# High parts of v and of the softmax factors made on ScalarE and stored, in place of masks on VectorE and raw copies

## The chip, the cores and the metric

One core of a Trainium2 chip. The metric is the device time of one execution in microseconds (us), as the median of several runs. Five engines run side by side, each with a queue of its own: TensorE (PE in the profile), VectorE (DVE), ScalarE (ACT), GpSimd (POOL) and SyncE (SP). SyncE only issues DMAs here; GpSimd issues DMAs and clears a few tiles.

## The reference

An attention with compressed keys and values for 8 batches, 8 heads, 576 positions and 64 columns a head, and behind it a block in which 128 of the 576 positions of each batch pass through two matrix products:

```
a    = softmax(phi, over the 576 positions)       # 32 columns a head
k_m  = sum over s of a[s, m] * k[s, d]
v_m  = sum over s of a[s, m] * v[s, d]
attn = softmax(q @ k_m.T / sqrt(64)); x = attn @ v_m, heads side by side (512 columns)
score = x @ w_gate; the 128 rows of largest score of a batch:
out  = x, and on those rows x + sigmoid(score) * (relu(x @ w1) @ w2)
```

## The kernel before

**Staging.** For each batch a chain of VectorE and ScalarE instructions computes the softmax factors a from phi (`softmax`; chain 0 takes batches 0, 2, 4, 6, 7, chain 1 takes 1, 3, 5). `keys` turns them by TensorE into `aS`, splits them, stores the parts to the scratch tensor `aparts`, and sums k_m. `split_v` does the same for v: 32 jobs of 128x576 values, four to a batch, each with a load (L531), a split and a store to the scratch tensor `vparts`. The sum v_m needs exact products from a TensorE that reads float32r, so both operands stand there in two parts, high and low, on partitions of their own.

**Pieces.** v_m is summed by `values` (L739) in 114 pieces of 12 positions. Up to four batches share a piece, 32 partitions each; `FIRST` says at which piece a batch begins, and each runs over 48 pieces: batches 0 to 3 begin at 0, 6, 12, 18, batches 4 to 7 at 48, 54, 60, 66. A piece needs its factors (`a_loader`, L658 on SyncE's queue, into one of three tiles `a_flat`), their widening to blocks of heads (`widener`, four instructions, L717 on VectorE or L719 on ScalarE, into one of two tiles `a_rows`), and its values with both parts (`v_loader`, L694 on the Pool queue, into one of three tiles `v_rows`). From piece 66 on, `values` begins a pair of pieces only when both are there.

**Behind the pieces.** When a batch's last piece is done its sum is turned (L757), and `attention` runs: `centre`, `scores`, `attend` (its first result of the products L929) and `rank`, which finds the 128 rows (L1033). Each of these four is open to one batch at a time. `forward` then gathers the rows, turns them (L1100), multiplies them (L1120, L1138) and writes them back.

**What sets the order.** All jobs are Python generators. `in_order_of_time` runs them against a model of the engines (class `Plan`) and so fixes, ahead of time, the order of the instructions on every queue. A change of one step can so reorder all that follows. On the chip each queue runs in that order, and each instruction waits for what it needs.

**The splits.** In `split_v` the low part of v is v less v with its lowest 12 bits masked away (L548, L550, both VectorE), and it is stored by the Pool queue (L553). The high part isn't computed: `v_copier` copies v itself from HBM to HBM on SyncE's queue (L675, six DMAs in three parts), and TensorE reads it as float32r. `v_loader` waits for both. In `keys` the high part of a batch's factors is a mask too (L593), then the low part a subtraction (L595), once for each half of the heads, and both are stored by the Pool queue (L601).

Of the kernel before, what the change touches and what calls it, by code (L numbers as in the profile page):

```python
# [10 lines left out]
F32 = mybir.dt.float32  # L11
F16 = mybir.dt.float16
F32R = mybir.dt.float32r
BF16 = mybir.dt.bfloat16
I32 = mybir.dt.int32
I16 = mybir.dt.int16
AF = mybir.ActivationFunctionType
ALU = mybir.AluOpType
# [3 lines left out]
P = 128  # L22
NC = 6
T = 12
FIRST = [0, 6, 12, 18, 48, 54, 60, 66]


LOG2E = 1.44269504088896341
# [161 lines left out]
def kernel(  # L190
# [304 lines left out]
    def phi_loader():  # L495
        for b in range(1, B):
            while b > 2 and b - 3 not in turned_away:
                yield lambda: b - 3 in turned_away
            if b == 2:
                yield 20e3  # L500
            load_phi(b)
            yield
# [18 lines left out]
    def split_v():  # L521
        jobs = [(b, g, c) for b in range(B) for c in range(VC) for g in range(NG)]
        asked = deque()

        def view(x, c):
            return x.rearrange("j (c x s) d -> c x j (s d)", c=VC, s=VX)[c]

        def ask():
            b, g, c = jobs[len(done) + len(asked)]
            vb = ex.tile([P, VX * Dh], F32, name="vb", bufs=3)  # L530
            nc.sync.dma_start(  # L531
                out=vb, in_=view(v[g, b % SET, :, first(b) * T:first(b) * T + S], c))
            asked.append((vb, plan.end))

        done, stored = [], [0.0, 0.0]
        yield 8e3
        ask()
        yield
        while len(done) < len(jobs):
            yield max(stored[-2], (8.0 + 7 * len(done)) * 1e3)  # L540
            while len(asked) < 2 and len(done) + len(asked) < len(jobs):
                ask()
            b, g, c = jobs[len(done)]
            vb, at = asked.popleft()
            yield at
            done.append((b, g, c))
            lo = ex.tile([P, VX * Dh], F32, name="vlo", bufs=2)
            nc.vector.tensor_single_scalar(lo.bitcast(I32), vb.bitcast(I32), -4096,  # L548
                                           op=ALU.bitwise_and)
            nc.vector.tensor_sub(lo, vb, lo)  # L550
            yield
            c0 = first(b) * T
            nc.gpsimd.dma_start(out=view(vparts[g, b % SET, :, 0, c0:c0 + S], c), in_=lo)  # L553
            stored.append(plan.end - 2000.0)
            split[b] = split[b][0] + 1, plan.end

# [2 lines left out]
    def keys():  # L559
        for b in range(B):  # L560
            aS = []
            waiting = deque()

            def settle():
                bk, g, c0 = waiting.popleft()
                copy(aS[g][:, :, c0:c0 + 3],
                     bk([PT, 3, P]).rearrange("p c (j m) -> p j c m", m=M))
                bk.give()

            for g in range(NG):  # L570
                while (b, g) not in soft:
                    yield lambda: (b, g) in soft
                yield soft[b, g][1]
                aS.append(ex.tile([PT, NPR, NC, M], F32, name="aS", bufs=2))
                a = soft[b, g][0].rearrange("p (x c) -> p c x", c=NC)
                for c0 in range(0, NC, 3):
                    bk = yield from take()
                    for c in range(3):
                        nc.tensor.transpose(out=bk([PT, 3, P])[:, c], in_=a[:, c0 + c],  # L579
                                            identity=ident)  # L580
                    waiting.append((bk, g, c0))
                    if len(waiting) > 1:
                        settle()
                    yield
            settle()
            turned_away.append(b)
            yield
            c0 = first(b) * T
            made = []
            for g in range(NG):  # L590
                lo = ex.tile([PT, NPR, NC, M], F32, name="alo", bufs=2)
                hi = ex.tile([PT, NPR, NC, M], F32, name="ahi", bufs=2)
                nc.vector.tensor_single_scalar(hi.bitcast(I32), aS[g].bitcast(I32), -4096,  # L593
                                               op=ALU.bitwise_and)
                nc.vector.tensor_sub(lo, aS[g], hi)  # L595
                made.append((lo, hi, plan.end))
            kc = work.tile([P, P], F32, name="kc", bufs=1)
            for g in range(NG):
                yield made[g][2]
                for part, src in enumerate(made[g][:2]):  # L600
                    nc.gpsimd.dma_start(  # L601
                        out=aparts[part, g, b % SET, :, c0:c0 + S]
                            .rearrange("j (p c) m -> p j (c m)", c=NC),
                        in_=src.rearrange("p j c m -> p j (c m)"))
            written[b] = plan.end
            for g in range(NG):
                bk = None
                for h in range(2):
                    while (b, g, h) not in ks:
                        yield lambda: (b, g, h) in ks  # L610
                    kb, at = ks[b, g, h]
                    yield at
                    if bk is None:
                        bk = yield from take()
                        km = bk([P, Dh])
                    for c in range(h * NC // 2, (h + 1) * NC // 2):
                        for j in range(NPR):
                            nc.tensor.matmul(out=km[j * M:(j + 1) * M], lhsT=aS[g][:, j, c],  # L618
                                             rhs=kb[:, j, c % (NC // 2)],
                                             start=(c == 0), stop=(c == NC - 1))  # L620
                    eaten.append(plan.end)
                yield
                copy(kc[:, g * Dh:(g + 1) * Dh], km)
                bk.give()
            bk = yield from take()
            nc.tensor.transpose(out=bk([P, P]), in_=kc, identity=ident)
            yield
            copy(kT[b].rearrange("p j m -> p (j m)"), bk([P, P]))
            bk.give()
            keyed[b] = plan.end  # L630
# [33 lines left out]
            flat.append(max(ends))  # L664
            yield plan.t

    copied = []

    def v_copier():
        yield 12.0 * 1e3  # L670
        edges = [0] + [24, 60] + [COLS // T]
        for c0, c1 in zip(edges, edges[1:]):
            for g in range(NG):
                x, y = (t.rearrange("b j s d -> (b j) (s d)")[:, c0 * T * Dh:c1 * T * Dh] for t in (vparts[g, :, :, 1], v[g]))
                nc.sync.dma_start(out=x, in_=y)  # L675
            copied.extend([plan.end] * (c1 - c0))
            yield plan.t + 40.0 * 1e3

    def v_loader():
        for ch in range(COLS // T):  # L680
            b = live(ch)[-1]
            while split[b][0] < NG * VC or len(copied) <= ch:
                yield lambda: split[b][0] == NG * VC and len(copied) > ch
            yield max(split[b][1], copied[ch])
            while ch - NV >= len(used_up) or len(flat) < ch:
                yield lambda: ch - NV < len(used_up) and len(flat) >= ch
            if ch >= NV:
                yield used_up[ch - NV]
            ends = []
            for g, (r0, r1) in ((g, r) for g in range(NG) for r in slots(ch)):  # L690
                plan.last = None
                src = vparts[g, r0:r1, :, :, ch * T:(ch + 1) * T].rearrange("b j w s d -> (b j w) (s d)")
                n = (r1 - r0) * NPR * 2
                nc.gpsimd.dma_start(  # L694
                    out=v_rows[ch % NV].bitcast(F32)[32 * r0 + g:32 * r1:2, g]
                        .rearrange("p s d -> p (s d)"),
                    in_=src.unsqueeze(1).to_broadcast([n, 2, T * Dh]))
                ends.append(plan.end)
            v_loaded.append(max(ends))
            yield plan.t  # L700
# [26 lines left out]

    def values():
        for ch in range(COLS // T):
            last = min(ch + 1 - ch % 2, COLS // T - 1) if ch >= 66 else ch  # L730
            while last >= min(len(widened), len(v_loaded)):
                yield lambda: last < min(len(widened), len(v_loaded))
            yield max(widened[last], v_loaded[last])
# [423 lines left out]
    def load_weights():  # L1157
# [24 lines left out]
    in_order_of_time(plan, [  # L1182
        (lambda: ahead(0), chain([[0, 2, 4, 6, 7], [1, 3, 5]][0], 0)), (lambda: ahead(1), chain([[0, 2, 4, 6, 7], [1, 3, 5]][1], 1)),
        (0.5 * 1e3, keys()), (0.0 * 1e3, split_v()),
        (0.0, phi_loader()), (0.0, k_loader()), (0.0, q_loader()), (0.0, a_loader()), (0.0, v_loader()), (0.0, v_copier()), (0.0, widener()),
        (0.0 * 1e3, values()), (0.0 * 1e3, attentions(0)), (0.0 * 1e3, attentions(1)),
        (None and None * 1e3, forward(B * nt)), (0.0, load_weights())])

# [51 lines left out]
```

## Time and profile before

| | us |
|---|---|
| median of 3 runs | 726.15 (725.95 to 727.72) |
| the profiled execution | 725.9 |
| its span in the trace | 724.0 |
| busy: VectorE | 567.1 |
| busy: TensorE | 465.0 |
| busy: ScalarE | 392.6 |
| busy: GpSimd | 216.6 |

The shares are means over stages with different limits. What counts is which engine is full in which stretch, and what the others wait for there. A queue with idle time costs nothing as long as nobody waits for it.

### The profile page before, as it was taken

How to read it: one execution, taken by the hardware profiler on the slowest of the kernel's cores; microseconds unless marked ns; L12 is line 12 of the kernel's file. 1: busy time of each engine (PE TensorE's matmuls, PEld its weight loads, DVE VectorE, ACT ScalarE, POOL GpSimd, SP SyncE). 2: the span in 40 equal slices, each digit the busy share in tenths (PEclk: the TensorE clock that was granted, in tenths of full speed). 3: DMA queues.
4: the chain of work that ended last, by engine and by line, in shares of the span. 5: the costliest groups of instructions: out<-in, count | busy, mean ns of one | idle time of the engine just before them, and what ended most of it. 6: DMA issues, size and time to landing. Idle time of an engine off the chain costs nothing.

```text
span 724.0 us, 18212 instructions
## 1 busy us (share of the span) xinstructions
PE 465.0 (64%) x7130; PEld 382.4 (53%) x7130; DVE 567.1 (78%) x990; ACT 392.6 (54%) x710; POOL 216.6 (30%) x387
## 2 busy tenths in 40 slices
PE   0002156074262474765668878999999999899990
PEld 0002045073261463654557677887878887686660
DVE  4999999999989996877988789879635877978000
ACT  3544664586462995867964376564646573243100
POOL 5001321431333241442332524244344331211100
PEclk9999999999975696998898999999999999999995
DMA  9613696776677686888987977887655543212000
GB/s 297 222 47 119 188 319 192 243 210 204 206 224 237 210 272 207 236 271 279 269 267 223 304 238 212 253 258 231 204 178 160 170 147 117 78 52 76 30 14 19
DMA packets 68109, 139.12 MB, mean 192 GB/s; under 512 B 13648, under 2 KB 46416, under 8 KB 67792
## 3 DMA queue, kind: packets, MB, share of 16 engines
q1 hardware_dynamic: 48752, 67.60, 31.4%
q0 software_dynamic: 19264, 70.28, 29.8%
q8 instruction: 58, 0.95, 0.6%
q14 instruction: 35, 0.29, 0.1%
HBM read 107.41 MB, written 41.62 MB: 206 GB/s over the span
## 4 chain that ended last, share of the span: by engine, by line
PE 33%; DMA 17%; DVE 13%; ACT 9%; SPq 6%; issue 5%; POOL 1%; ACTq 0%; DVEq 0%
PE acc L739 11%; DMA a_flat<-aparts 10%; ACT a_rows L719 6%; SPq L658 6%; PE acc L1138 4%; PE bank L1120 4%; PE acc L1120 3%; PE bank L1138 3%; DMA qb<-in_qT 2%; DMA aparts<-ahi 2%; DMA w<-in_w 2%; PE bank L904 1%; PE bank L1028 1%; PE bank L918 1%; DVE marks L1009 1%
## 5 line engine op out<-in xcount | busy, mean ns | idle before, releaser
L739 PE MATMUL acc<-v_rows,a_rows 32*128 32x256 f32 x4608 | 219.8, 312 | 97.8 <-ACT a_rows L719 77.8
L739 PEld LDWEIGHTS acc<-v_rows,a_rows 32*128 32x128 f32 x4608 | 201.5, 214 | 117.5 <-ACT a_rows L719 85.5
L719 ACT ACTIVATE a_rows<-a_flat,block_of 128x384 fp32r<-128x384 f32 x325 | 174.1, 604 | 91.2 <-PE acc L739 40.0
L694 POOL DMA_DIRECT2D v_rows<-vparts x228 | 128.5, 567 | 222.0 <-PE acc L739 199.5
L717 DVE TENSOR_SCALAR a_rows<-a_flat,block_of 128x384 fp32r<-128x384 f32 x131 | 49.9, 420 | 46.8 <-DMA a_flat<-aparts 31.2
L579 PE MATMUL bank<-ident,ph 128*96 128x128 f32 x96 | 20.4, 359 | 73.3 <-DVE ph L476 73.3
L553 POOL DMA_DIRECT2D vparts<-vlo x32 | 18.6, 582 | 122.1 <-DVE vlo L550 122.1
L579 PEld LDWEIGHTS bank<-ident,ph 128*96 128x96 f32 x96 | 14.3, 190 | 77.1 <-issue 59.5
L618 PE MATMUL bank<-kb,aS 96*32 96x64 f32 x768 | 22.5, 282 | 42.9 <-DMA kb<-in_k 42.9
L618 PEld LDWEIGHTS bank<-kb,aS 96*32 96x32 f32 x768 | 17.5, 148 | 48.3 <-issue 27.2
L1009 DVE SCALAR_TENSOR_TENSOR marks<-row,tg,wide 128x576 bf16<-128x576 f32 x40 | 32.7, 818 | 7.4 <-ACT row L993 5.7
L962 POOL DMA_DIRECT2D out<-xj x24 | 16.4, 683 | 61.4 <-DVE less L1014 25.6
L1120 PE MATMUL bank<-xeT,w 128*128 128x128 f32 x256 | 32.8, 281 | 1.7 <-ACT xeT L1104 1.7
L1120 PE MATMUL acc<-xeT,w 128*128 128x128 f32 x256 | 31.7, 279 | 2.0 <-ACT xeT L1104 2.0
L1120 PEld LDWEIGHTS bank<-xeT,w 128*128 128x128 f32 x256 | 29.9, 192 | 4.2 <-ACT xeT L1104 2.1
L1005 ACT ACTIVATE marks<-row,tg 128x576 bf16<-128x576 f32 x40 | 31.0, 776 | 1.8
L1120 PEld LDWEIGHTS acc<-xeT,w 128*128 128x128 f32 x256 | 29.6, 192 | 4.1 <-ACT xeT L1104 3.0
L1138 PE MATMUL bank<-w,hT 128*128 128x512 f32 x64 | 30.4, 605 | 0.0
L1138 PE MATMUL acc<-w,hT 128*128 128x512 f32 x64 | 29.5, 600 | 0.0
L473 DVE SCALAR_TENSOR_TENSOR ph<-rh,sm,ph 128x576 f32<-128x576 f16 x32 | 26.0, 813 | 2.8 <-ACT rh L462 2.5
L968 DVE TENSOR_TENSOR prod<-xj,wg 128x512 f32<-128x512 f32 x40 | 27.4, 686 | 0.4
L971 DVE TENSOR_REDUCE four<-prod 128x128 f32<-128x512 f32 x40 | 27.2, 681 | 0.6
(163 smaller groups left out, 924.9 us busy)
## 6 DMA issues: line engine op xcount, KB each, us to landing
v_rows<-vparts POOLq DMA_DIRECT2D x156, 192.0 KB
a_flat<-aparts SPq DMA_DIRECT2D x312, 48.0 KB
vb<-in_v SPq DMA_DIRECT2D x32, 288.0 KB
kb<-in_k SPq DMA_DIRECT2D x32, 288.0 KB
vparts<-vlo POOLq DMA_DIRECT2D x32, 288.0 KB
qb<-in_qT SPq DMA_DIRECT2D x16, 576.0 KB
out<-xj POOLq DMA_DIRECT2D x16, 512.0 KB
vparts<-in_v SPq DMA_DIRECT2D x2, 2592.0 KB
```

The lines of the kernel that those rows point to most:

```text
L579: nc.tensor.transpose(out=bk([PT, 3, P])[:, c], in_=a[:, c0 + c], identity=ident)
L618: nc.tensor.matmul(out=km[j * M:(j + 1) * M], lhsT=aS[g][:, j, c], rhs=kb[:, j, c % (NC // 2)], start=(c == 0), stop=(c == NC - 1))
L658: nc.sync.dma_start(out=a_flat[ch % NF][32 * r0 + 2 * t + g:32 * r1:4] .rearrange("p s m -> p (s m)"), in_=src[:, ch * T * M:(ch + 1) * T ...
L694: nc.gpsimd.dma_start(out=v_rows[ch % NV].bitcast(F32)[32 * r0 + g:32 * r1:2, g] .rearrange("p s d -> p (s d)"), in_=src.unsqueeze(1).to_b ...
L717: nc.vector.tensor_scalar_mul(ar[:, :, j], src, block_of[:, j:j + 1])
L719: nc.scalar.activation(ar[:, :, j], src, AF.Copy, scale=block_of[:, j:j + 1])
L739: nc.tensor.matmul(out=accs[b % SET][:, :2 * P].rearrange("p (r g d) -> p r g d", g=NG, d=Dh), lhsT=ar[p, s].rearrange("p j m -> p (j m)") ...
L968: nc.vector.tensor_mul(prod, x[:, c], wg)
L1005: nc.scalar.activation(sign, row, AF.Sign, bias=g, scale=-1.0, accum_out=less[:, c:c + 1])
L1009: nc.vector.scalar_tensor_tensor(out=cmp, in0=row, scalar=g, in1=wide[:, off:off + S], op0=ALU.is_equal, op1=ALU.mult, accum_out=equal[:, ...
L1120: nc.tensor.matmul(out=bk([P, 4, P])[:, f, :n], lhsT=w1_sb[d][:, (f0 + f) * P:(f0 + f + 1) * P], rhs=xeT[:, d, :n], start=(d == 0), stop=( ...
L1138: nc.tensor.matmul(out=ps[:n], lhsT=hT[:, f, :n], rhs=w2_sb[f], start=(f == 0), stop=(f == KF - 1))
```

## The change

`split_v` writes the high part of v by a ScalarE copy into a float32r tile, subtracts it from v in place on VectorE, and stores both parts by the Pool queue. The mask, the low tile and the copies from HBM to HBM are gone, and `v_loader` waits for the split alone. Jobs of v are due 6.5 us apart instead of 7. In `keys` the high part of the factors is a ScalarE copy into float32r, and the subtraction is planned as a step of its own, after the copies of both halves. Batch 1 begins at piece 10 instead of 6, batch 5 at 58 instead of 54; the count of pieces stays 114. Pieces are begun in pairs from piece 60 instead of 66.

```diff
-FIRST = [0, 6, 12, 18, 48, 54, 60, 66]
+FIRST = [0, 10, 12, 18, 48, 58, 60, 66]
...
-            yield max(stored[-2], (8.0 + 7 * len(done)) * 1e3)
+            yield max(stored[-2], (8.0 + 6.5 * len(done)) * 1e3)
...
-            lo = ex.tile([P, VX * Dh], F32, name="vlo", bufs=2)
-            nc.vector.tensor_single_scalar(lo.bitcast(I32), vb.bitcast(I32), -4096,
-                                           op=ALU.bitwise_and)
-            nc.vector.tensor_sub(lo, vb, lo)
+            hi = ex.tile([P, VX * Dh], F32R, name="vhi", tag="vlo", bufs=2)
+            copy(hi, vb)
+            yield
+            nc.vector.tensor_sub(vb, vb, hi.bitcast(F32))
             yield
             c0 = first(b) * T
-            nc.gpsimd.dma_start(out=view(vparts[g, b % SET, :, 0, c0:c0 + S], c), in_=lo)
+            for w, src in enumerate((vb, hi.bitcast(F32))):
+                nc.gpsimd.dma_start(out=view(vparts[g, b % SET, :, w, c0:c0 + S], c), in_=src)
...
-                hi = ex.tile([PT, NPR, NC, M], F32, name="ahi", bufs=2)
-                nc.vector.tensor_single_scalar(hi.bitcast(I32), aS[g].bitcast(I32), -4096,
-                                               op=ALU.bitwise_and)
+                hi = ex.tile([PT, NPR, NC, M], F32R, name="ahi", bufs=2)
+                copy(hi, aS[g])
+                made.append((lo, hi.bitcast(F32), plan.end))
+            for g in range(NG):
+                lo, hi, at = made[g]
+                yield at
                 nc.vector.tensor_sub(lo, aS[g], hi)
-                made.append((lo, hi, plan.end))
+                made[g] = lo, hi, plan.end
...
-    copied = []
-
-    def v_copier():
...
-            while split[b][0] < NG * VC or len(copied) <= ch:
-                yield lambda: split[b][0] == NG * VC and len(copied) > ch
-            yield max(split[b][1], copied[ch])
+            while split[b][0] < NG * VC:
+                yield lambda: split[b][0] == NG * VC
+            yield split[b][1]
...
-            last = min(ch + 1 - ch % 2, COLS // T - 1) if ch >= 66 else ch
+            last = min(ch + 1 - ch % 2, COLS // T - 1) if ch >= 60 else ch
```

## Rows read from the trace of the kernel before

**Rows 1.** Stretches: busy us (count) PE, PEld, DVE, ACT, POOL; clock, DMA, GB/s.

```profile
24.00:229.00 205.00, 71.66 (x819) 62.33 (x819) 197.27 (x244) 111.53 (x156) 48.42 (x81) 0.95 0.63 193
244.00:378.00 134.00, 86.24 (x2077) 76.72 (x2070) 114.77 (x161) 105.18 (x179) 47.30 (x83) 0.85 0.83 254
378.00:456.00 78.00, 63.95 (x1276) 53.03 (x1261) 64.89 (x157) 45.84 (x108) 29.77 (x53) 0.91 0.79 243
456.00:672.00 216.00, 209.33 (x2775) 166.89 (x2776) 158.82 (x394) 108.15 (x245) 70.66 (x118) 1.00 0.50 158
672.00:706.00 34.00, 32.39 (x177) 22.24 (x175) 1.82 (x3) 3.58 (x6) 2.96 (x3) 1.00 0.07 24
```

**Rows 2.** VectorE, 20 to 240 us, its largest wait: us in total, times, longest.

```profile
DVE vlo L548 <- DMA vb<-in_v: 2.5, 2, 1.7
```

**Rows 3.** Order of time round batch 3: start, us, engine, line, operation, idle before.

```profile
228.05 0.95 DVE L595 TENSOR_TENSOR alo<-aS,ahi 96x768 f32<-96x768 f32 x1
...
230.01 0.87 POOL L601 DMA_DIRECT2D aparts<-ahi  x1
...
241.25 4.16 ACT L719 ACTIVATE a_rows<-a_flat,block_of 128x384 fp32r<-128x384 f32 x8 [1.02 <-DMA a_flat<-aparts]
...
243.44 2.94 PE L739 MATMUL acc<-v_rows,a_rows 32*128 32x256 f32 x48 [13.12 <-ACT a_rows L719]
```

**Rows 4.** Instructions grouped by shape: count, busy us, mean ns of one, idle before.

```profile
L553 POOL DMA_DIRECT2D vparts<-vlo x32 | 18.6, 582 | 122.1 <-DVE vlo L550 122.1
...
L548 DVE TENSOR_SCALAR vlo<-vb 128x576 int32<-128x576 int32 x32 | 14.7, 458 | 2.5 <-DMA vb<-in_v 2.5
...
L462 ACT ACTIVATE rh<-ph,sm 128x576 f16<-128x576 f32 x16 | 11.4, 762 | 4.9 <-DVE sm L458 4.9
...
L394 ACT ACTIVATE rh<-ph 128x1152 int16<-128x1152 f32 x8 | 9.3, 1162 | 33.7 <-DVE ph L392 33.7
...
L593 DVE TENSOR_SCALAR ahi<-aS 96x768 int32<-96x768 int32 x16 | 8.8, 549 | 0.0
```

**Rows 5.** VectorE's masks alone in the front: L548, then L593, busy us (count).

```profile
24.00:229.00 205.00, 13.31 (x29) 0.95 0.63 193
...
24.00:230.00 206.00, 4.40 (x8) 0.94 0.63 193
```

**Rows 6.** DMA queues of the page: packets, MB, share of 16 engines' span.

```profile
q1 hardware_dynamic: 48752, 67.60, 31.4%
q0 software_dynamic: 19264, 70.28, 29.8%
```

**Rows 7.** Order of time: sums read (L757), an attention's products, last rank and round.

```profile
378.88 0.26 ACT L757 ACTIVATE turned<-acc 128x128 f32<-128x128 f32 x1
...
402.76 0.28 ACT L757 ACTIVATE turned<-acc 128x128 f32<-128x128 f32 x1 [1.13 <-PE acc L739]
...
421.59 0.19 DVE L929 TENSOR_SCALAR rd<-bank 128x40 f32<-128x40 f32 x1
...
561.32 0.26 ACT L757 ACTIVATE turned<-acc 128x128 f32<-128x128 f32 x1
...
580.52 0.26 ACT L757 ACTIVATE turned<-acc 128x128 f32<-128x128 f32 x1
...
671.24 0.16 DVE L1033 TENSOR_SCALAR idx<-bank 128x1 int32<-128x1 f32 x1 [1.77 <-PE bank L1028]
...
690.07 0.60 PE L1100 MATMUL acc<-ident,xe 128*128 128x128 f32 x4
```

**Rows 8.** Waits of SyncE's queue at the loads of v, 20 to 245 us.

```profile
SPq L531 <- DVE vlo L550: 56.7, 12, 24.7
...
SPq L531 <- DMA vparts<-in_v: 13.1, 2, 8.1
```

**Rows 9.** Wait of the Pool queue for pieces, 20 to 245 us.

```profile
POOL v_rows L694 <- PE acc L739: 31.2, 8, 9.1
```

**Rows 10.** The page's first part: busy us, share of the span, instructions.

```profile
PE 465.0 (64%) x7130; PEld 382.4 (53%) x7130; DVE 567.1 (78%) x990; ACT 392.6 (54%) x710; POOL 216.6 (30%) x387
```

More of the change, by code (lines that the diff above doesn't have):

```diff
@@ L665, in a_loader @@
             yield plan.t
-    copied = []
-    def v_copier():
[L670 to L677, printed above, removed]
     def v_loader():
@@ L1184 @@
         (0.5 * 1e3, keys()), (0.0 * 1e3, split_v()),
-        (0.0, phi_loader()), (0.0, k_loader()), (0.0, q_loader()), (0.0, a_loader()), (0.0, v_loader()), (0.0, v_copier()), (0.0, widener()),
+        (0.0, phi_loader()), (0.0, k_loader()), (0.0, q_loader()), (0.0, a_loader()), (0.0, v_loader()), (0.0, widener()),
         (0.0 * 1e3, values()), (0.0 * 1e3, attentions(0)), (0.0 * 1e3, attentions(1)),
```

## The prediction, made before the changed kernel was run

> **What bounds the kernel now.** I read the stretches of the span first [rows 1]. They show three regimes. From 24 to 229 us VectorE is busy 197.27 of 205 us, TensorE only 71.66 and ScalarE 111.53. From 244 to 456 us nothing is full: TensorE is busy 86.24 of 134 and then 63.95 of 78 us. From 456 to 706 us TensorE is busy 209.33 of 216 and 32.39 of 34 us: it works off a backlog, and what it finds to do is always there. So the end is set by the time at which TensorE becomes full, and that by how early the front gets through.
>
> What holds the front is read from the waits of VectorE between 20 and 240 us: its largest wait of all there adds to 2.5 us [rows 2]. VectorE is simply full, with the softmax of the factors, with the splitting of v and of the factors into parts. The order of time round batch 3 shows how that reaches TensorE [rows 3]: the last low part of the factors of batch 3 is subtracted at 228.05, its parts leave on the Pool queue at 230.01, the widening begins at 241.25, and at 243.44 TensorE begins piece 18, the first that has batch 3, after 13.12 us of waiting. Pieces before it run as soon as their batch is there and wait for the next one, so piece 18 is the gate of the front. Everything behind it (96 pieces, eight attentions, eight rounds of the block) follows on.
>
> **VectorE's masks go.** By shape, a mask of v is 0.458 us (L548, 32 times) and a mask of a factor tile 0.549 us (L593, 16 times) [rows 4]. In the stretch that ends with batch 3's factors, 29 of the first (13.31 us) and 8 of the second (4.40 us) lie on the full VectorE [rows 5]: together 17.7 us. The new spacing of the jobs of v, 6.5 for 7 us, doesn't raise the 29: the front ends earlier by about as much as the jobs are nearer (211 - 8 over 6.5 is 31.2 and 229 - 8 over 7 is 31.6, by the due times alone). The subtractions stay as they are.
>
> **ScalarE gets the copies.** No row of before is a plain copy of these shapes. For 128x576 the bounds are half of the 1.162 us that 1152 columns take (L394), 0.58, and the 0.762 us of the scaled conversion of 576 columns (L462) [rows 4]. I take 0.70, nearer to L462, which has the same width. For 96x768 they are two thirds of 1.162, 0.775, and 0.762 plus 192 columns of the slope between the two rows (0.400 / 576 each), 0.895; I take 0.84. In the front that is 29 x 0.70 + 8 x 0.84 = 27.0 us (23.0 to 29.3), so that ScalarE goes from 111.5 of 205 to some 138.5 of 188 us, 74%: room, but less of it. Over the whole kernel it is 32 x 0.70 + 16 x 0.84 = 35.8 us added on ScalarE, for 14.7 + 8.8 = 23.5 us removed from VectorE [rows 4]: 12.3 us more of engine time. A copy of v also waits for its load, and behind it on ScalarE stand widenings and softmax steps; that the loads come late cost VectorE 2.5 us so far [rows 2], and I leave that as it is.
>
> Each subtraction now waits for a ScalarE result. Behind a waiting subtraction on VectorE stand the softmax steps of both chains, and for these ScalarE and the next batch wait. The bound is zero if the planner always puts other work between, as it does now, and otherwise what such waits cost now: all idle time of VectorE in the front is 205 - 197.3 = 7.7 us [rows 1], and softmax has some 50 steps there that take a ScalarE result (ten in each of some five batches), so at most 0.15 us each, 5.7 us for 37 more. I take 2.0, since the named waits are so small [rows 2]. For the factors of batch 3 the mask in line with its subtraction becomes a copy on another queue: from 1 us earlier to 2 us later; I take 1.0 later. Piece 18 then starts 17.7 - 2.0 - 1.0 = 14.7 us earlier, near 229.
>
> A rule that speaks against this is in the Trainium skill, Perfetto Trace Analysis, section Optimizing Scalar/DVE Operations: where VectorE has a fast mode for an operation it is the quicker place, though with VectorE saturated some work may go to ScalarE. By the first half alone the kernel would come out 12.3 us later, at 738.4; by the second it gains. The trace agrees with the second for the front, and leaves it open behind 244 us.
>
> **Raw copies go, stored high parts come.** Six copies from HBM to HBM on SyncE's queue give way to 32 more stores of 288 KB on the Pool's. The copies move 114 pieces x 12 rows x 64 x 4 bytes x 32 = 11.2 MB, the stores 9.4 MB. SyncE's queue has 31.4% of the 16 engines' span for 67.60 MB, 3.36 us a MB; the Pool's 29.8% for 70.28 MB, 3.07 us a MB [rows 6]. That is -37.7 + 29.0 = -8.7 us of transfer time, nearly all inside a front that is 63% loaded [rows 1]: I count it at nothing, between -2 and +2 us, as no wait of VectorE rests on it. On the Pool, issuing 32 more stores at 0.582 us [rows 4] is 18.6 us; Pool has 48.42 of 205 us busy there [rows 1], and the issue time is hidden by that. Its order isn't free, see the second rival.
>
> **Behind piece 18.** Between 244 and 378 us VectorE (114.77 of 134) and ScalarE (105.18 of 134) are nearly equal [rows 1]. Four batches of factors are split there: 8 x 0.549 = 4.4 us leave VectorE, 8 x 0.84 = 6.7 us come to ScalarE. The bounds are -4.4 and +6.7; I take nothing, as the planner gives each widening to the freer of the two. From 456 us on TensorE has the same work, so it ends earlier by what it begins earlier.
>
> **The pieces.** Batch 1 runs over pieces 10 to 57 and batch 5 over 58 to 105, four later than before. At the front that is covered by the waits for batches 2 and 3. Its price is at the ends of those batches: batch 1's sum is ready at 378.88 and batch 2's, six pieces on, at 402.76, so four pieces are 15.9 us; for batch 5 (561.32, and 580.52 six pieces on) 12.8 us [rows 7]. Cover for batch 1: its attention begins its products at 421.59, when batch 0's has let go, while the sum was there 42.7 us before. Cover for batch 5: the last batch's rank is known at 671.24, and TensorE only takes its round at 690.07, 18.8 us later [rows 7]. Both covers exceed the delays, so zero; without them it would be 15.9 and 12.8 us. Waiting for pairs from piece 60 instead of 66 moves six pieces and I count zero, within one piece's time either way (15.9 / 4 = 4.0 us).
>
> **The sum.** 725.9 us for the profiled execution (span 724.0 and 1.9 around it) - 14.7 = 711.2. The median is 726.15, 0.25 above that execution: 711.5 for the median.
>
> **The rivals.** First, the gain is lost before 456 us. Batch 1's delay of 15.9 us cancels the 14.7 us at its attention, and if TensorE's fullness hangs on that attention and not on the pieces, the end is 726.15 - 14.7 + 15.9 = 727.4 at most; half of it, 719, if batch 0 fills in. For it speaks the 64 of 78 us that TensorE is busy just then [rows 1]; against it the cover of 42.7 us.
>
> Second, slower: the queues couple. The tile of v is now overwritten by its own low part and is free only when the Pool's store has landed; the next load of v into it stands on SyncE's queue, and behind that stand the loads of the factors for the pieces. Now the same load waits for the subtraction, 56.7 us in the front [rows 8], while the Pool's queue waits 31.2 us for pieces on TensorE, in eight waits of up to 9.1 us [rows 9]. If those eight fall between a store and the SyncE load that needs it, and all reach the path, the time is 726.15 - 17.7 + 31.2 = 739.7. It decides once more than 17.7 us of the 31.2 come ahead of the loads for pieces 12 and 18. Against it: three tiles of v give a store nearly three jobs' time to land, and with the raw copies a wait of 13.1 us leaves SyncE [rows 8]. The Trainium skill, DMA: Bandwidth & Descriptors, section Issuing engine by pattern, would keep plain stores on SyncE's path, which it calls generally faster; the rows' 3.07 us a MB don't show that.
>
> Third, ScalarE becomes the bound: its copies wait behind widenings that wait for TensorE, and the subtractions with them. With all 12.3 us of added engine time on the path the time is 726.15 + 12.3 = 738.4; it decides where ScalarE, at 78% between 244 and 378 us, is later than VectorE at most pieces. With the 5.7 us and 2 us bounds of the front alone it would be 726.15 - 17.7 + 7.7 = 716.2, still faster.
>
> **How the numbers follow.** Forecast, 702 to 720: 0.70. The first rival 0.14, of which 0.04 at 720 to 724, 0.08 within 0.3% and 0.02 above. The second 0.11, the third 0.05, of which 0.01 each within 0.3%. About 0.3%, 2.2 us, is what a measurement of this kernel can tell from no change. Faster 0.74, same 0.10, slower 0.16. The low end of the range is all 23.5 us of removed masks with nothing given back, 702.6, rounded to 702; the high end takes in the first rival and a quarter of the second, 730.
>
> **What would show it.** After: VectorE busy near 567.1 - 23.5 = 543.6 us and ScalarE near 392.6 + 35.8 = 428.4 [rows 10]; piece 18 beginning near 229 us; TensorE full from about 442; batch 3's factors leaving near 215. Wrong, if piece 18 starts at 240 or later (second rival: SyncE's loads of v waiting for the Pool's stores), if it starts early and TensorE fills no earlier (first rival), or if VectorE shows waits for ScalarE's copies of more than 6 us (third).

## The result, and the profile after

The changed kernel takes 706.76 us as the median of 4 runs (705.59 to 709.69), beside 726.93 us (725.95 to 729.38) for the kernel before: a ratio of 0.972 with an interval of 0.968 to 0.977, or 20.2 us less. The forecast was 711.5: the direction is right, and 4.7 us are missing from it. The two profiled executions differ by as much: span 703.9 for 724.0 us. Executions more than 1.5% above the fastest of the same kernel are left out of every median and ratio from here on.

Stretches of the kernel after, with the columns of [rows 1]: busy us (and count) of TensorE, its weight loads, VectorE, ScalarE and GpSimd, then clock, DMA share and GB/s.

```profile
24.00:215.00 191.00, 74.58 (x771) 65.13 (x771) 180.83 (x210) 132.74 (x191) 63.79 (x110) 1.00 0.65 208
...
244.00:378.00 134.00, 86.07 (x2032) 75.25 (x2031) 109.38 (x166) 97.66 (x167) 46.23 (x82) 0.85 0.84 255
378.00:442.00 64.00, 50.20 (x1047) 41.76 (x1042) 48.08 (x121) 36.68 (x84) 26.52 (x47) 0.89 0.80 244
442.00:660.00 218.00, 210.97 (x2834) 167.91 (x2835) 165.32 (x409) 109.46 (x250) 71.85 (x118) 1.00 0.52 161
```

The three regimes are still there, only earlier. Up to 215 us VectorE is busy 180.83 of 191 us, and from 442 us on TensorE is full, 210.97 of 218, where it was full from 456 [rows 1]. Over the same time, from 440 to 460 us, it is busy 19.15 of 20 us, and 16.49 in the kernel before.

The order of time round batch 3 in the kernel after, to be held against [rows 3]:

```profile
213.89 0.94 DVE L599 TENSOR_TENSOR alo<-aS,ahi 96x768 f32<-96x768 f32 x1
...
218.32 0.68 POOL L605 DMA_DIRECT2D aparts<-ahi  x1
...
228.82 3.65 ACT L711 ACTIVATE a_rows<-a_flat,block_of 128x384 fp32r<-128x384 f32 x7 [1.16 <-DMA a_flat<-aparts]
...
231.00 1.23 PE L731 MATMUL acc<-v_rows,a_rows 32*128 32x256 f32 x16 [8.12 <-ACT a_rows L711]
```

The last subtraction begins at 213.89 for 228.05 us, 14.2 earlier; piece 18 at 231.00 for 243.44, 12.4 earlier. In a second profiled execution of the changed kernel (e8, below) piece 18 is at 228.63, 14.8 earlier.

From the gate the gain goes through to the end almost whole. Order of time in the kernel before, its last product, its last result and its last store:

```profile
705.57 0.20 PE L1191 MATMUL bank<-good,ones 128*1 128x8 f32 x2
705.68 0.75 DVE L1144 SCALAR_TENSOR_TENSOR ye<-acc,gr,xe 128x512 f32<-128x512 f32 x1 [14.65 <-PE acc L1138]
...
706.71 0.97 POOL L1149 DMA_INDIRECT out<-ye,idx  x1 [14.41 <-DVE any_bad L1197]
```

And in the kernel after, with the last rank ahead of it:

```profile
662.70 0.16 DVE L1025 TENSOR_SCALAR idx<-acc 128x1 int32<-128x1 f32 x1 [0.55 <-PE acc L1020]
...
694.69 0.96 POOL L1141 DMA_INDIRECT out<-ye,idx  x1 [14.42 <-DVE any_bad L1189]
```

The last store is issued 12.0 us earlier. But the span is 20.1 us shorter. The other 8.1 us lie behind the last store: from its issue to the end of the span are 724.0 - 706.71 = 17.3 us before and 703.9 - 694.69 = 9.2 us after. The instructions of the line that ends the program, on the Pool queue (durations ns min/median/max, then first and last start in us), say what it is. The profile calls them DRAIN; what they wait for, no row shows. Before:

```profile
L1236 POOLq DRAIN  x3: 46/108/9133, 713.8 to 723.4; - x3
```

After:

```profile
L1228 POOLq DRAIN  x3: 46/108/2441, 700.6 to 703.6; - x3
```

The longest of three drains of the Pool queue took 9.133 us before and takes 2.441 us now: 6.7 of the 8.1 us. Of the remaining 1.4 us, 1.2 are that the drains begin 5.9 us behind the last store for 7.1.

**The new work in size.** Instructions of the kernel after by shape: count, busy us, mean ns, idle before and what ended it, as [rows 4].

```profile
L550 DVE TENSOR_TENSOR vb<-vb,vhi 128x576 f32<-128x576 f32 x32 | 24.0, 749 | 0.6 <-ACT vhi L548 0.5
L548 ACT ACTIVATE vhi<-vb 128x576 fp32r<-128x576 f32 x32 | 21.5, 672 | 17.0 <-DMA vparts<-vhi 10.9 <-DMA vb<-in_v 4.7 <-issue 1.2
...
L594 ACT ACTIVATE ahi<-aS 96x768 fp32r<-96x768 f32 x16 | 12.5, 834 | 0.0
```

VectorE's whole wait for the copies of v is 0.5 us, once. The first part of the page and its queues, as [rows 10] and [rows 6]:

```profile
PE 467.3 (66%) x7130; PEld 384.7 (55%) x7130; DVE 550.2 (78%) x962; ACT 412.6 (59%) x738; POOL 234.3 (33%) x419
...
q0 software_dynamic: 21952, 79.72, 34.4%
q1 hardware_dynamic: 48432, 56.39, 27.8%
```

### The profile page after: what moved, and what is told of

Same layout as the page of the kernel before. It is cut to its first block, busy times and chain, and to the rows that moved or that the text cites. A ratio compares the mean times of both kernels' runs of the same rounds, so it can differ in the third digit from the quotient of the medians.

```text
span 703.9 us, 18360 instructions
## 1 busy us (share of the span) xinstructions
PE 467.3 (66%) x7130; PEld 384.7 (55%) x7130; DVE 550.2 (78%) x962; ACT 412.6 (59%) x738; POOL 234.3 (33%) x419
## 3 DMA queue, kind: packets, MB, share of 16 engines
q0 software_dynamic: 21952, 79.72, 34.4%
## 4 chain that ended last, share of the span: by engine, by line
PE 39%; DMA 17%; DVE 17%; ACT 9%; issue 8%; SPq 6%; POOL 2%; ACTq 0%; DVEq 0%; POOLq 0%
PE acc L731 14%; DMA a_flat<-aparts 8%; PE bank L1112 6%; SPq L662 6%; DMA kb<-in_k 4%; PE acc L1130 4%; PE bank L1130 4%; ACT a_rows L711 3%; PE bank L910 2%; DMA qb<-in_qT 2%; PE acc L1112 2%; DVE ph L473 1%; DVE vb L550 1%; PE bank L1020 1%; PE acc L896 1%
## 5 line engine op out<-in xcount | busy, mean ns | idle before, releaser
L731 PE MATMUL acc<-v_rows,a_rows 32*128 32x256 f32 x4608 | 222.7, 314 | 92.5 <-ACT a_rows L711 67.9
L731 PEld LDWEIGHTS acc<-v_rows,a_rows 32*128 32x128 f32 x4608 | 204.8, 216 | 111.9 <-ACT a_rows L711 76.7
L711 ACT ACTIVATE a_rows<-a_flat,block_of 128x384 fp32r<-128x384 f32 x305 | 164.9, 605 | 106.6 <-DMA a_flat<-aparts 54.1
L709 DVE TENSOR_SCALAR a_rows<-a_flat,block_of 128x384 fp32r<-128x384 f32 x151 | 57.6, 420 | 61.5 <-DMA a_flat<-aparts 29.0
L554 POOL DMA_DIRECT2D vparts<-vb x32 | 18.7, 585 | 113.4 <-DVE vb L550 108.1
L580 PEld LDWEIGHTS bank<-ident,ph 128*96 128x96 f32 x96 | 14.7, 191 | 76.2 <-issue 58.0
L1112 PE MATMUL bank<-xeT,w 128*128 128x128 f32 x384 | 48.1, 280 | 3.4 <-ACT xeT L1096 2.8
L1112 PEld LDWEIGHTS bank<-xeT,w 128*128 128x128 f32 x384 | 44.5, 192 | 7.1 <-ACT xeT L1096 4.2
L548 ACT ACTIVATE vhi<-vb 128x576 fp32r<-128x576 f32 x32 | 21.5, 672 | 17.0 <-DMA vparts<-vhi 10.9
L963 DVE TENSOR_REDUCE four<-prod 128x128 f32<-128x512 f32 x40 | 27.2, 680 | 0.6
L1136 DVE SCALAR_TENSOR_TENSOR ye<-acc,gr,xe 128x512 f32<-128x512 f32 x4 | 3.0, 747 | 30.0 <-PE acc L1130 30.0
```

The source lines that it names most:

```text
L709: nc.vector.tensor_scalar_mul(ar[:, :, j], src, block_of[:, j:j + 1])
L711: nc.scalar.activation(ar[:, :, j], src, AF.Copy, scale=block_of[:, j:j + 1])
L731: nc.tensor.matmul(out=accs[b % SET][:, :2 * P].rearrange("p (r g d) -> p r g d", g=NG, d=Dh), lhsT=ar[p, s].rearrange("p j m -> p (j m)") ...
L1112: nc.tensor.matmul(out=bk([P, 4, P])[:, f, :n], lhsT=w1_sb[d][:, (f0 + f) * P:(f0 + f + 1) * P], rhs=xeT[:, d, :n], start=(d == 0), stop=( ...
```

## The experiments

Theories before the runs. A: relief of the full VectorE up to piece 18 is the gain, as predicted. B: it is the copies from HBM to HBM, whose traffic went away. C: it is the new places of batches 1 and 5 (`FIRST`) and of the pairs. The 8 us behind the last store needed a theory of their own. They ran in three groups, each beside runs of the kernel before on the same chip, whose medians are 728.50 us for e1 to e4, 726.54 for e5 to e8 and 728.74 for e9 to e12. Ratios are against the kernel before in the same group; they aren't the plain quotients of these medians. Where an experiment says "in unchanged order", its instruction was added without the planner knowing of it, so that all queues keep their order; elsewhere the planner made a new one.

**e1 to e4: one part at a time, re-planned.** e1 is the kernel before with the ScalarE parts alone.

```diff
-            nc.vector.tensor_single_scalar(lo.bitcast(I32), vb.bitcast(I32), -4096, ...)
-            nc.vector.tensor_sub(lo, vb, lo)
+            hi = ex.tile([P, VX * Dh], F32R, name="vhi", tag="vlo", bufs=2)
+            copy(hi, vb)
+            yield
+            nc.vector.tensor_sub(vb, vb, hi.bitcast(F32))
...
+                copy(hi, aS[g])
```

> The kernel before with the high parts made on ScalarE and nothing else: the low part is subtracted in place and stored, the raw copies from HBM to HBM stay, batches, spacing and pairs stay. Here TensorE still reads the raw v as its high part, which need not be the rounded one that was subtracted; that part of the sum is changed. Theory one (VectorE's masks held the front): piece 18 starts 10 to 14 us earlier than the 243.44 us of before, and the last instruction of work comes as much earlier, so 711 to 717 us. Theory two (the copies from HBM to HBM held it): 724 to 730 us, piece 18 later than 240 us. Theory three (8 us of the gain lie behind the last store, in the Pool queue's drain at the end of the program, 9.1 us before and 2.4 after): the drain here tells whether it goes with the stores; with the 9.1 us drain the time is 714 to 716, with the short one 706 to 709.

e2 is the changed kernel with the masks on VectorE again, stored as they are.

```diff
-            copy(hi, vb)
+            nc.vector.tensor_single_scalar(hi.bitcast(I32), vb.bitcast(I32), -4096, ...)
...
-                copy(hi, aS[g])
+                nc.vector.tensor_single_scalar(hi.bitcast(I32), aS[g].bitcast(I32), -4096, ...)
```

> The changed kernel with the high parts masked on VectorE again, in tiles of their own, and still stored; everything else as changed. Theory one: piece 18 back at 240 to 246 us (231.00 after), the time 718 to 724 us with a short drain. Theory two (copies and stores carry the gain): 705 to 710 us, piece 18 at 231 to 234 us. Theory three: the drain stays near 2.4 us if the 32 further stores on the Pool queue decide it, so that the time is 8 us under what piece 18 alone would give.

e3 is the changed kernel with the copies of v from HBM to HBM back, in place of the stored high part.

```diff
-            for w, src in enumerate((vb, hi.bitcast(F32))):
-                nc.gpsimd.dma_start(out=view(vparts[g, b % SET, :, w, c0:c0 + S], c), in_=src)
+            nc.gpsimd.dma_start(out=view(vparts[g, b % SET, :, 0, c0:c0 + S], c), in_=vb)
...
+    def v_copier(): ...   # as before
```

> The changed kernel with the raw copies from HBM to HBM back in place of the stored high parts of v (TensorE again reads the raw v as its high part, so that part of the sum is changed). Theory one: within 3 us of the changed kernel up to the last store, piece 18 at 229 to 234 us. Theory two: piece 18 at 238 us or later, 716 us or more. Theory three: the drain is near 9 us if it goes with the number of stores on the Pool queue, and the time is 713 to 717 us although piece 18 is early; near 2.4 us otherwise and 704 to 709 us.

e4 is the kernel before once more.

> The kernel before, once more, for the drain at the end of the program alone. If it belongs to the kernel: 8.5 to 9.5 us again, 725 to 729 us. If it is an accident of one execution: anything from 2 us, and the span shorter by as much.

Measured: e1 735.10 us, ratio 1.009 (1.006 to 1.013); e2 1.014 (1.005 to 1.022) from two executions of 727.55 and 734.29 us; e3 740.22, 1.017 (1.010 to 1.023); e4 724.61, with the drain of 9.133 us again. In e1 and e3 the sum v_m is a changed one, as their texts say; the work on the queues is as described. Neither ScalarE's copies without the stores (e1, e3) nor the stores without ScalarE's copies (e2) gain anything; together they gain 20 us. So neither A nor B holds as a term that can be added by itself. The table shows where, for the kernels whose order was planned anew, one profiled execution a row (start of piece 18, the last subtraction of the jobs of v, how many of these begin behind the start of piece 18, the time from there to piece 48, the last store issued, and the time from there to the end of the span):

| | piece 18 | last job of v | jobs behind piece 18 | piece 18 to 48 | last store | behind it |
|---|---|---|---|---|---|---|
| before | 243.4 | 240.7 | 0 | 113.1 | 706.7 | 17.3 |
| before (e4) | 243.0 | 240.6 | 0 | 108.8 | 705.4 | 17.4 |
| after | 231.0 | 230.0 | 0 | 116.0 | 694.7 | 9.2 |
| after (e8) | 228.6 | 227.2 | 0 | 112.2 | 695.4 | 9.4 |
| e1 | 231.6 | 284.2 | 6 | 126.7 | 716.2 | 17.6 |
| e2 | 238.6 | 269.2 | 3 | 122.7 | 715.7 | 10.1 |
| e3 | 234.3 | 277.3 | 5 | 128.4 | 722.1 | 17.8 |
| e10 | 225.4 | 239.9 | 2 | 124.2 | 702.6 | 9.4 |
| e11 | 222.5 | 284.1 | 7 | 131.8 | 721.2 | 8.8 |

In e1 the gate opens 11.9 us earlier, as A says: VectorE's relief is real with the copies in place. But the jobs of v now end at 284 us, 53 us behind the gate instead of ahead of it, and the stretch from piece 18 to 48 takes 13.6 us more than before. What TensorE waits for in that stretch of e1 (us in total, times, longest):

```profile
PE acc L742 <- ACT a_rows L722: 39.0, 16, 13.7
PE bank L621 <- DMA kb<-in_k: 9.4, 4, 3.3
PE acc L742 <- DMA v_rows<-vparts: 8.9, 2, 7.0
```

And from piece 18 to 48 in the kernel before:

```profile
PE acc L739 <- ACT a_rows L719: 36.9, 19, 13.1
PE acc L739 <- DVE a_rows L717: 10.2, 2, 9.7
...
PE bank L618 <- DMA kb<-in_k: 1.8, 1, 1.8
```

For widenings TensorE waits no longer in e1 (39.0 + 2.2 on VectorE for 47.1), but for the transfers of keys and of values 18.3 us where the kernel before has 1.8. The transfers alone don't make the difference, though. In the same stretch of the changed kernel (e8) they are waited for too:

```profile
PE acc L731 <- ACT a_rows L711: 27.2, 12, 9.2
PE acc L731 <- DMA v_rows<-vparts: 6.6, 2, 3.8
PE bank L622 <- DMA kb<-in_k: 4.9, 2, 3.3
```

That is 11.5 us, and the stretch is no longer than before. Against e8, e1 waits 6.8 us more for transfers and 11.4 more for widenings (39.0 + 2.2 for 27.2 + 2.6). Nor is the whole loss in that stretch: from piece 48 to the last store e1 takes 357.9 us, for 350.1 in the kernel before and 354.6 in e8. So late jobs of v became a suspect, and so did the price of the copies, which a plan of its own can hide. The next runs kept the order.

**e5 and e6: masks alone and copies alone, in unchanged order.** e5 is the changed kernel with 48 masks on VectorE whose result nobody reads. e6 has the six copies of v, to a scratch tensor that nobody reads, issued on SyncE's queue at the 1st, 7th and 13th job. By the trace that is in pairs from 7.3, 66.0 and 118.5 us; the kernel before issues its own from 3.9, 12.5 and 92.0 us, so e6 prices them at other places. e7 has one copy of 48 KB in their place, to see whether such a copy by its mere presence lengthens the end; e8 is the changed kernel as it is.

```diff
+            dead = ex.tile([P, VX * Dh], I32, name="dead", bufs=1)
+            tc.nc.vector.tensor_single_scalar(dead, vb.bitcast(I32), -4096, op=ALU.bitwise_and)
             nc.vector.tensor_sub(vb, vb, hi.bitcast(F32))
...
+                dead = ex.tile([PT, NPR, NC, M], I32, name="deada", bufs=1)
+                tc.nc.vector.tensor_single_scalar(dead, aS[g].bitcast(I32), -4096, op=ALU.bitwise_and)
                 nc.vector.tensor_sub(lo, aS[g], hi)
```

> The changed kernel with the 48 masks back on VectorE as dead work: each writes a tile that nothing reads, right ahead of its subtraction, and the planner isn't told, so the order of all other instructions on every queue is that of the changed kernel. It takes apart the cost of the masks from that of another order. Theory one (VectorE full in the front, what is saved there goes to the end): piece 18 starts 29 x 0.46 + 8 x 0.55 = 17.7 us less the 9 us that VectorE stood idle there, so 9 to 18 us after the 231.00 of the changed kernel, and the time is 716 to 725 us. Rival (the gain is the new order's and the copies', the masks were hidden): piece 18 within 4 us, the time 705 to 711 us.

```diff
+            for c0, c1, n in ((0, 24, 1), (24, 60, 7), (60, COLS // T, 13)):   # e7: ((0, 1, 1),)
+                if len(done) == n:
+                    for g0 in range(NG):                                       # e7: range(1)
+                        ...   # x = vraw[g0], y = v[g0], columns c0 to c1
+                        tc.nc.sync.dma_start(out=x, in_=y)
```

> The changed kernel with the six copies of v from HBM to HBM back as dead transfers into a scratch tensor that nothing reads, issued on SyncE's queue with the first, seventh and thirteenth job of v; the planner isn't told, so the order of all other instructions is that of the changed kernel. Theory of the order (the copies cost the kernels that have them 8 us in the drain at the end, and nothing else by their traffic): piece 18 and piece 48 within 3 us of 231.0 and 347.0, the last store of the block within 3 us of 694.7, then 17 to 18 us to the end instead of 9.2, so 713 to 717 us. Rival (the traffic itself delays the front): piece 18 at 236 us or later, 718 us or more. Second rival (the drain goes with the number of stores on the Pool queue): 9 to 10 us behind the last store.

> The changed kernel with one short dead copy from HBM to HBM (one piece of v, 48 KB, on SyncE's queue) and nothing else. If the drain at the end grows by the mere presence of a copy from HBM to HBM: 17 to 18 us behind the last store and 713 to 716 us. If it grows with their bytes or number: 9 to 11 us behind the last store and 705 to 709 us.

> The changed kernel once more, beside the three before it on the same chip: 704 to 710 us, 9 to 10 us behind the last store if that belongs to the kernel and not to one execution.

Measured: e8 705.29 us, ratio 0.970 (0.965 to 0.975); e5 718.78, 0.989 (0.985 to 0.992); e6 726.80, 0.999 (0.997 to 1.002); e7 704.83, 0.972 (0.964 to 0.980). The masks cost 718.78 - 705.29 = 13.5 us. The prediction had 14.7. Piece 18 of e5, then of e8, in their orders of time:

```profile
243.69 2.72 PE L735 MATMUL acc<-v_rows,a_rows 32*128 32x256 f32 x44 [11.49 <-ACT a_rows L715]
```

```profile
228.63 3.77 PE L731 MATMUL acc<-v_rows,a_rows 32*128 32x256 f32 x61 [9.19 <-ACT a_rows L711]
```

They are 15.1 us apart at the gate, and at the last store, 710.5 for 695.4, 15.2: in these two executions what VectorE is given back at the front comes out at the end without loss.

The copies cost 726.80 - 705.29 = 21.5 us in this order and at these places. That is B's price here, and it exceeds A's. Waits of e6 from 20 to 232 us, the time that the changed kernel needs up to piece 18:

```profile
DVE vb L557 <- ACT vhi L555: 24.0, 4, 14.9
...
ACT vhi L555 <- DMA vparts<-vhi: 18.4, 3, 13.3
ACT vhi L555 <- DMA vb<-in_v: 17.4, 2, 16.8
```

And e6's piece 18:

```profile
249.84 2.51 PE L738 MATMUL acc<-v_rows,a_rows 32*128 32x256 f32 x40 [8.21 <-ACT a_rows L718]
```

Loads and stores of v land late beside the copies, ScalarE waits for them up to 16.8 us, and VectorE behind ScalarE 24.0 us in four waits, where the changed kernel has one of 0.5. Subtractions that wait for ScalarE are what the third rival feared, but here transfers set them off. Batch 3's last subtraction moves from 211.1 to 233.3 us, piece 18 from 228.6 to 249.8. One small copy (e7) costs nothing, so it isn't the mere presence of such a copy. The kernel before doesn't pay the 21.5 us as waits (VectorE's largest is 2.5 [rows 2]), and its plan has a hole there: between its jobs at 98.15 and 117.95 us no subtraction of v stands, while the changed kernel has 3 in that time, with copies gone. The two other kernels that were planned with the copies have the hole at the same place (e1 from 96.85 to 119.05 us, e3 from 96.83 to 119.03), and e2 and e10, planned without them, have none. That points to a price which sits in the order; no run took the hole alone away.

**e9: the 8 us at the end.** In e1 and e3, which store one part, the time behind the last store is 17.6 and 17.8 us, in e2, e5, e6 and e7, which store both, 9.0 to 10.1; e6 has the copies as well. So it goes with the stores on the Pool queue. e9 is the kernel before with 32 further stores of the low part, to a tensor that nobody reads, in unchanged order.

```diff
             nc.gpsimd.dma_start(out=view(vparts[g, b % SET, :, 0, c0:c0 + S], c), in_=lo)
+            tc.nc.gpsimd.dma_start(out=view(vraw[g, b % SET, :, c0:c0 + S], c), in_=lo)
```

> The kernel before with 32 dead stores on the Pool queue: each low part of v is stored a second time into a scratch tensor that nothing reads; the planner isn't told, so all other instructions keep their order. So far the kernels with 32 further stores (five of them, with and without copies from HBM to HBM) end 9.0 to 10.1 us after the block's last store is issued, the four without end 17.3 to 17.8 us after it. If the drain goes with the stores on the Pool queue: 9 to 10.5 us, the last store issued within 4 us of the 706.7 of before, and 716 to 722 us although nothing else is gained. If it goes with something else in the changed kernels: 17 to 18 us and 725 to 730 us.

Measured: 719.82 us, ratio 0.987 (0.981 to 0.994). More work, and faster. The drain of e9, and that of e1, which has the kernel before's count of stores:

```profile
L1239 POOLq DRAIN  x3: 46/108/2441, 715.8 to 718.8; - x3
```

```profile
L1239 POOLq DRAIN  x3: 108/193/8888, 723.6 to 733.4; - x3
```

The last store of e9 is issued at 709.9 us, 3.2 later than before, with piece 18 3.4 later (246.89); behind it there are 9.2 us for 17.3. The stores alone bring the short drain. In all profiled executions read here the longest drain was 8.9 to 9.1 us with 387 instructions on GpSimd, and 2.0 to 3.1 us with 419.

**e10 to e12: the places of the batches, late jobs, and tiles.** e10 puts `FIRST` back. e11 is the changed kernel with jobs of v due 8.5 us apart, and nothing else: a test of late jobs. e12 gives the changed kernel a fourth tile of v and a third tile of the high part: if stores on the Pool queue hold SyncE's queue (the second rival), this must gain. Three tiles of `forward` share this memory and get one more as well.

```diff
-FIRST = [0, 10, 12, 18, 48, 58, 60, 66]
+FIRST = [0, 6, 12, 18, 48, 54, 60, 66]
```

> The changed kernel with batches 1 and 5 at pieces 6 and 54 again. By the prediction both delays are covered and the move is worth nothing: 703 to 709 us, piece 18 at 228 to 232 us. Rival (the later start of batch 1 gives the front its gain, because its pieces no longer crowd between batches 1 and 2): 710 us or more. Rival the other way (the attention of batch 1 or 5 was held back): 703 us or less.

```diff
-            yield max(stored[-2], (8.0 + 6.5 * len(done)) * 1e3)
+            yield max(stored[-2], (8.0 + 8.5 * len(done)) * 1e3)
```

> The changed kernel with the jobs of v due every 8.5 us instead of 6.5, so that the last are at 271 us or later by the plan, some seven of them behind piece 18. In the kernels with the copies the jobs ran late too, to 277 and 284 us, and the stretch from piece 18 to piece 48 took 127 and 128 us instead of 112 to 116. If late jobs slow that stretch (their loads and stores stand on the queues that feed the pieces): piece 18 at 222 to 228 us, the stretch 120 us or more, 710 us or more in all. If they don't: the stretch 112 to 117 us, and 700 to 706 us.

```diff
-            vb = ex.tile([P, VX * Dh], F32, name="vb", bufs=3)
+            vb = ex.tile([P, VX * Dh], F32, name="vb", bufs=4)
...
-            hi = ex.tile([P, VX * Dh], F32R, name="vhi", tag="vlo", bufs=2)
+            hi = ex.tile([P, VX * Dh], F32R, name="vhi", tag="vlo", bufs=3)
```

> The changed kernel with four tiles for v instead of three and three for its high part instead of two, which takes away what the loads of v on SyncE's queue (86.3 us in the front) and the copies on ScalarE (14.4 us) wait for: the Pool's stores. The second rival's coupling, if it still costs anything: piece 18 at 227 us or earlier and 700 to 704 us. If the jobs have time enough: within 2 us of the changed kernel's 705.3 us.

Measured: e10 712.07 us, ratio 0.973 (0.967 to 0.979); e11 730.55, 1.003 (0.999 to 1.007); e12 704.06, 0.964 (0.959 to 0.969). Of e12 only the time is used.

e11 opens the gate at 222.5 us, 6.1 us earlier than e8, and ends 25 us later. Fewer jobs in the front are the wrong relief: seven of them come back behind the gate. The stretch from piece 18 to 48 in e8, then in e11, columns as above:

```profile
228.60:340.80 112.20, 75.74 (x1744) 66.57 (x1744) 101.14 (x132) 89.35 (x143) 40.98 (x73) 0.83 0.89 267
```

```profile
222.50:354.30 131.80, 85.84 (x1795) 75.86 (x1796) 122.54 (x166) 99.51 (x161) 49.17 (x86) 0.72 0.90 283
```

VectorE is busy 122.54 us there for 101.14 and nearly full, and TensorE takes 85.84 us for 75.74 with about as many products, at a granted clock of 0.72 for 0.83 (means over times at 2.4 and at 1.2 GHz). Which of the two lengthens it, and how much, the runs don't part. Another part of the loss lies behind piece 48: from there to the last store e11 takes 366.9 us for 354.6 in e8, and from 455 to 670 us TensorE isn't full, 196.50 of 215 us; no row says why. e1's stretch has e8's clock, 0.83, and VectorE at 103.91 of 126.7 us, so neither of the two shows there. What is common to e1, e2, e3 and e11, and absent before and after, is that jobs of v run 31 to 62 us past the gate (e10 lies between, at 14.5). The table has the stretch to piece 48 at 108.8 to 116.0 us with no job behind the gate, 122.7 to 124.2 with two or three, and 126.7 to 131.8 with five to seven. e11 shows that jobs made late, with no other edit, lose the whole gain; by which wait, stays open.

e12 is 1.2 us below e8, and by the ratios, 0.964 for 0.970 with intervals that overlap, at most a few us faster. So the wait of SyncE's queue for the Pool's stores,

```profile
SPq L531 <- DMA vparts<-vb: 83.5, 13, 35.4
```

in the kernel after from 20 to 230 us, where it was 56.7 us for the subtraction [rows 8], holds up little or nothing of the path.

## Why the prediction was right, and where it wasn't

**What bounds the kernel** was right: VectorE full up to piece 18, then pieces at their own pace, then TensorE. From piece 18 to the last store there are 463.3 us before and 463.7 after (466.7 in e8).

**The masks** were right in mechanism and size: 17.7 - 2.0 - 1.0 = 14.7 us at the gate; measured 13.5 us of time and 15.1 at the gate in unchanged order (e5 less e8), 12.4 and 14.8 at the gate in two executions of the changed kernel. The Trainium skill, Perfetto Trace Analysis, section Optimizing Scalar/DVE Operations, allows ScalarE for such work where VectorE is saturated. The trace agrees: a mask on VectorE is 458 ns [rows 4] and the copy on ScalarE 672, and still e8 is 13.5 us faster than e5.

**The copies on ScalarE** were sized well: 672 ns for 700, 834 for 840. The 2.0 us of waits for them were 0.5. Whole-kernel sums missed what the planner would do: VectorE 550.2 us for a forecast of 543.6, ScalarE 412.6 for 428.4. The planner gave 20 more widenings to VectorE (151 for 131), 20 x 0.420 = 8.4 us, and as many fewer to ScalarE, 20 x 0.605 = 12.1 us. That none of this lies on the path is read only from the 463.3 and 463.7 us above. The other signs named came as forecast: piece 18 at 231.0 for 229, TensorE full from 442, batch 3's factors leaving at 214 to 218 for 215.

**Raw copies against stores: this step failed.** The transfer time was about right, by the queues' shares (61.2% of 724.0 and 62.2% of 703.9 us) 443.1 less 437.8 = 5.3 us for a forecast of 8.7. In the kernel after a MB takes 0.344 x 703.9 / 79.72 = 3.04 us on the Pool's queue and 3.47 on SyncE's, for different transfers. The Trainium skill, DMA: Bandwidth & Descriptors, section Issuing engine by pattern, gives simple stores to SyncE's path, which it calls "generally faster". The trace of after doesn't show that either. But "I count it at nothing" was not right: the test "no wait of VectorE rests on it" was made on a trace whose order had been planned round these copies. Put beside an order that isn't, they cost 21.5 us (e6), and in e3, whose order is planned round them, five jobs of v run behind the gate and the time is 740.22. So ScalarE's copies alone, which the prediction's sum says give 14.7 us, make the kernel 0.9% slower (e1). The forecast of the whole came out because the change has both parts, and because the new order keeps every job of v ahead of piece 18 (last at 230.0, piece 18 at 231.0). The sentence that the spacing "doesn't raise the 29" didn't see that this is a condition of the gain: where the spacing is so wide that seven jobs come behind, in e11 with 8.5 us, 25 us are lost. What the step from 7 to 6.5 us gives by itself, no run shows.

**The end of the program: this step failed too.** The sum took everything behind TensorE's last product as fixed ("ends earlier by what it begins earlier"). 8.1 us of the 20.1 are there, in the drain, and come from the 32 stores on the Pool queue (e9), which the prediction had counted at zero. Of the sum's shortfall this is more than all: 14.7 forecast, 12.0 found at the last store, plus 8.1. The two misses pull opposite ways, 2.7 us too much at the last store and 8.1 too little behind it; that this brought the forecast within 4.7 us is luck.

**The pieces.** Batch 1's sum is read at 381.10 us, 2.2 later than before [rows 7] although the gate is 12.4 earlier: a delay of 14.6 us for the 15.9 forecast. Its attention's products come at 413.74 for 421.59, 7.9 us earlier; the last store is 12.0 earlier, so the rest isn't on the path. That the cover held shows in e10 as well: with batch 1 back at piece 6 its sum is read 5.4 us earlier than in e8 (370.85 for 376.29) and its products come no earlier (407.90 for 407.57). For batch 5 the last rank is known at 662.70 and TensorE takes its round at 678.06, 15.4 us later. Zero for `FIRST` isn't settled even so: e10 has the earlier gate (225.4 us) and a stretch behind it of 124.2 us for 112.2; it takes 712.07 beside 704.06 of e12 in the same group, and the ratios of e10 and of the changed kernel (0.973, and 0.970 to 0.972, each against the kernel before of its own group) can't be told apart. Between 0 and 8 us of the gain are its own. The pairs from piece 60 were changed back in no run.

**The rivals.** The first didn't come: TensorE is full from 442 us, as forecast for the gain. The second didn't come in the changed kernel (e12 leaves it a few us at most), though late transfers that hold the front are what e6 shows. The third didn't come: VectorE waits 0.5 us.

## What to carry to other kernels

Relief is worth counting on the engine that is full up to the gate, instruction by instruction: here the masks were forecast at 14.7 us and measured 13.5 to 15.1 in a held order. "Hidden" in a trace of a planned kernel means hidden by that plan, and a transfer or job that a plan leaves room for is free only as long as its place is; put the suspected cost in with the order held still before calling it zero. Read the time from the last store to the end as a part of the sum.

## What the hardware showed that was not expected

The drain of the Pool queue at the end of the program became 6 to 7 us shorter by 32 more stores on that queue, though the last of them is issued more than 400 us before the end. e9 shows that the stores bring it; why a larger count drains faster stays open, as no run varied it in smaller steps.
